# Projection pieces cut into single products between runs of scores, and one and a half value units in each run

## The chip, the core and the metric

The kernel runs on one core of a Trainium2 chip. The metric is the time of one execution on the device, in microseconds; lower is better. Before the change the median of three runs is 2965.22 us (2965.06 to 2965.87).

## The reference

Two layers, each of two parts, are applied to 2048 tokens of width 512, in fp32. The first part is attention with 32 query heads of width 16 that share one key head and one value head; the second sends the two tokens with the highest router score through a gated network and adds a layer norm of everything else.

```python
def _A_ref(x, wq, wk, wv, wo):
    q = (x @ wq).reshape(B, S, H, Dh).transpose(0, 2, 1, 3)
    k, v = x @ wk, x @ wv
    p = softmax(einsum("bhqd,bkd->bhqk", q, k) * Dh ** -0.5)
    return einsum("bhqk,bkd->bhqd", p, v).transpose(0, 2, 1, 3).reshape(B, S, H * Dh) @ wo

x = x + _A_ref(_layernorm(x), ...)          # layer 1
x = x + _B_ref(_layernorm(x), ...)          # two routed tokens through the gated network
x = x + _A_ref(_layernorm(x), ...)          # layer 2
x = x + _B_ref(_layernorm(x), ...)
```

## The kernel before

A layer is a stream of 512 steps. The 2048 tokens make four chunks of 512, the 32 heads make four groups of eight; a chunk and a group make one `p` (16 of them, 32 steps each), and each `p` has two units `u` of 16 steps. A unit is cut into blocks of query columns: two blocks of 8 steps for most units, four blocks of 4 steps for the first and the last unit of a layer (`cuts[u]`).

In each step the recording loop at the end of `layer` issues, for engine PE, four score matmuls of 512 columns (`scores`, L356), whose exponential ACT takes (L358), and four matmuls for the row maxima of queries that come 12 steps later (`max_mm`, L307), which DVE reduces (L309). Scores have three PSUM banks (`psS`), maxima four (`psM`), and the sum of values one (`psO`, tile `pO`).

Every three scores make a run (`RUN`). At the end of a run PE gets the value units that are ready (`pv_mm`, L375): a unit is the product of the exponentials of two scores with the values, four matmuls side by side of 32 output rows each, 256 columns wide. Since two scores make a unit, the runs have one and two units in turn. Behind them stands the held work whose step has come (`run(held.pop(0))`): `at(step, f, ...)` enters it in a table by step, and it is issued whole. fp32 matmuls show twice in the trace, so a unit is eight instructions there.

The projections are such held work. A query piece (`q_piece`) makes 128 tokens of the next `p`'s queries: four products (of four matmuls each, `by_columns`, L154) are summed in a score bank, ACT copies the sum to `qf` (L251), and GpSimd splits it into two parts for `q_stack`, which SP then sends to where scores and maxima read it. An output piece (`o_piece`) makes 128 by 128 of the output projection in the same way, four products from four head groups, and GpSimd adds it to the residual (L457, L458). Query pieces stand at steps 2 to 11 of each `p`; the 16 output pieces of a chunk at steps 14 to 28 of two consecutive `p` of the next chunk. When a chunk's pieces are done, statistics (`stats2`, L178), `norm2` on GpSimd, and `block_b` (L488, L491 on DVE, L493 on GpSimd) follow, and in the first layer the next layer's keys and values.

When a unit's block is summed, ACT copies it out of `pO` (L379). `z_move` to `z_mul` then carry the row sums through DRAM and divide by them. ACT, DVE and GpSimd take their work strictly in the order in which it was recorded.

Of the kernel before, what the change touches and what calls it, by code (L numbers as in the profile page):

```python
# [16 lines left out]
P = 128  # L17
# [35 lines left out]
def interleaved_layers(ctx, tc, x_in, wq, wkv, wo, w_r, w_gate, w_up, w_down, out):  # L53
# [95 lines left out]

    def by_columns(out, lhsT, rhs, start, stop):  # L150

        for j in range(4):
            r = slice(32 * j, 32 * (j + 1))
            nc.tensor.matmul(out[r], lhsT[:, r], rhs, start=start, stop=stop)  # L154

# [91 lines left out]
    def q_piece(G, w):  # L247
        q_proj(G, w)
        qh, ql = (a[:, w] for a in parts[G])
        qf = work.tile([P, P], F32, name="qf")  # L250
        nc.scalar.activation(qf, pqs.pop(G), AF.Copy, scale=DH ** -0.5)  # L251
        nc.gpsimd.tensor_copy(qh, qf)  # L252
        nc.gpsimd.tensor_tensor(ql, qf, qh.bitcast(F32), op=OP.subtract)  # L253

    def q_stack(G, s, w=slice(0, CW), parts_of=range(2 * NSLOT)):
        u = 2 * G + s
        if u not in q_st:
            q_st[u] = work.tile([P, 2, CW], FR, name="q_st", bufs=5)
        for i in parts_of:
            n, h = divmod(i, 2)  # L260
            r = s * HR + h * 32
            nc.sync.dma_start(q_st[u][h * HR + n * DH:h * HR + (n + 1) * DH, :, w].bitcast(F32),
                              parts[G][Q_SLOTS[n]][r:r + 32, w].bitcast(F32))

    def layer(li, src_d, dst_d, changed):
# [93 lines left out]

        def pv_mm(hs):  # L360
# [7 lines left out]
            if r == b == i == 0:  # L368
                po[u] = psO.tile([P, CW], F32, name="pO")
                so[u] = work.tile([P, CW], F32, name=f"so{u % 2}", bufs=6 - 5 * (u % 2))  # L370
            p = pr.pop(hs).rearrange("p h (k j n) -> p h k j n", k=nk, j=2)
            for k in range(nk):
                kt = r * nq + i * nk + k
                for j in range(4):
                    nc.tensor.matmul(po[u][32 * j:32 * (j + 1), b * w:(b + 1) * w],  # L375
                                     v_ext[:, kt, 1 - u % 2:33 - u % 2], p[:, j % 2, k, j // 2, :],
                                     start=kt == 0, stop=kt == KT - 1)
            if r == KT // nq - 1 and i == 1:
                nc.scalar.copy(so[u][:, b * w:(b + 1) * w], po[u][:, b * w:(b + 1) * w])  # L379
                return True  # L380
            return False

        zt, zc, on, on_last = {}, {}, {}, {}
# [34 lines left out]
        def z_last(i):  # L418
# [9 lines left out]
            if u not in zt:  # L428
                zt[u] = work.tile([P, CW], F32, name="so0", bufs=6)
            o = zt[u][:, w]  # L430
# [23 lines left out]
        def o_piece(i, w, gs):  # L454
            o_proj(i, w, gs)
            y = work.tile([P, OW], F32, name="qf")
            nc.scalar.copy(y, py.pop(i))  # L457
            nc.gpsimd.tensor_tensor(x1[i][:, w], x1[i][:, w], y, op=OP.add)  # L458

# [57 lines left out]
        for p in range(NCH * NG):  # L517
            e = 32 * p
            if p + 1 < NCH * NG:
                for n in range(4):  # L520
                    w = slice(n * P, (n + 1) * P)
                    at(e + T_Q + n * D_Q, q_piece, p + 1, w)
                for n in range(2 * NSLOT):
                    s, k = divmod(n, NSLOT)
                    at(e + T_ST + n, q_stack, p + 1, s, slice(0, CW), range(2 * k, 2 * k + 2))
                at(e + T_ST + 2 * NSLOT, parts.pop, p + 1)
            if p == 0:
# [8 lines left out]
            at(e + T_Z + 8, z_spread, u, range(2, 4))  # L536
            at(e + T_Z + 10, z_mul, u)

            if c == NCH - 1 and g == NG - 2:
                for n in range(4 * TPC):  # L540
                    i = c * TPC + n // 4
                    w = slice(n % 4 * OW, (n % 4 + 1) * OW)
                    if n % 4 == 0:
                        at(e + 4, load_x, i)
                    at(e + 14 + n, o_piece, i, w, range(NG - 1))
            if g < NG - 1:
                continue
            for n in range(TPC * 4):
                i = c * TPC + n // 4
                w = slice(n % 4 * OW, (n % 4 + 1) * OW)  # L550
                t = e + 32 * (n // 8) + T_O[n % 8]
                if n % 4 == 0:
                    at(e + 4, load_x, i)
                at(t, o_piece, i, w, range(NG))
                if n % 4 == 3:
                    at(t + 3, stats2, i)
            at(e + T_B[0] - 2, norm2, c)
            for b in range(TPC):
                i = c * TPC + b
                t = e + T_B[0] + T_B[1] * b  # L560
                at(t, block_b, i, nc.vector)
                at(t + 2, store_xl, i)
                at(t + 4, store_x, i)
                if li == 0:
                    t = e + T_N[0] + T_N[1] * b
                    at(t, next_x, i)
# [6 lines left out]
        def load_wd(n):  # L573
            rows = w_down[n * 2 * FS:(n + 1) * 2 * FS, :].rearrange("(k p) d -> p k d", p=FS)
            if n < 4:
                w = work.tile([P, 2, D], F32, name="q_st", bufs=5)
                nc.sync.dma_start(w[:FS], rows)
                wd.extend(w[:FS, k, :] for k in range(2))
            else:
                for k in range(2):  # L580
                    if n < 6:
# [21 lines left out]
        last = NU * KT  # L603
        for n in range(3):
            at(last - 24, load_wd, n)
        at(last - 24, load_wg, 0)
        at(last - 14, load_wd, 3)
        for n in range(4, 8):
            at(last - 13, load_wd, n)
# [32 lines left out]
        for t in range(-LEAD0, last):  # L642
# [5 lines left out]
            for i in range(4):  # L648
# [15 lines left out]
        while ready < 2 * last:  # L664
            pv_mm(ready)
            ready += 1
        while held:
# [7 lines left out]
        for k in range(1, NDC):  # L675
            load_wg(k)
        z_last(TPC - 1)
        finish_b(i - 1)
        o_proj(i, slice(0, D), [NG - 1])
        if nxt:  # L680
# [222 lines left out]
```

## Time and profile before

| | |
|---|---|
| median of three runs | 2965.22 us |
| the profiled execution's own time | 2968.59 us |
| its span, first to last instruction | 2966.5 us |
| mean granted TensorE clock | 0.971 |
| PE busy | 2879.7 us, 97% |
| DVE busy | 2669.2 us, 90% |
| ACT busy | 2295.9 us, 77% |
| GpSimd (POOL) busy | 378.8 us, 13% |

Matmuls are pipelined and their ends are modelled, so PE's busy time says little about how near it is to its limit; the starts of its groups say more. PEld is the weight load. In a table of stretches the columns after the stretch are the busy times of PE, PEld, DVE, ACT and POOL with their instruction counts, the granted clock, the share of the DMA engines and GB/s. In a timeline the first number is the start and the second the length of a merged group of `x` instructions.

### The profile page before, as it was taken

Reading aid. Unit: us, or ns where it says so; the run is one execution under the profiler, and the core shown is the slowest. Engines: PE = TensorE matmul, PEld = TensorE weight load, DVE = VectorE, ACT = ScalarE, POOL = GpSimd, SP = SyncE. Lnnn points to the kernel's source line nnn. Section 1 sums busy time; section 2 is a strip of 40 time slices with the busy share of each in tenths; the row PEclk is TensorE's granted clock in tenths of the full one; section 3 lists DMA queues with packets and bytes.
Section 4 is the critical chain, followed back from the end, with each engine's and each line's share of the span. In section 5 each row is a group of like instructions: output and inputs, shape, how many; then the busy total and the mean of one; then the engine's idle time right before and its main releaser. Section 6 shows DMA issues by size and latency. Waiting matters only on the chain. (4 is left out here: it accounts for less than half of the span.)

```text
span 2966.5 us, 82864 instructions
## 1 busy us (share of the span) xinstructions
PE 2879.7 (97%) x34503; PEld 1502.9 (51%) x34503; DVE 2669.2 (90%) x4616; ACT 2295.9 (77%) x4757; POOL 378.8 (13%) x973
## 2 busy tenths in 40 slices
PE   7999999999999999999979999999999999999997
PEld 4644445544555445544636444455445554455454
DVE  6999999998999999999559999999999999999993
ACT  2788888878888788887717888888788887888783
POOL 3000000121010211111320000001101111011102
PEclk8899999999999999999969999999999999999998
DMA  4000010010100101001310000100101001100122
GB/s 153 13 19 19 10 31 15 19 44 19 33 8 19 43 17 33 19 14 62 89 47 13 19 19 11 30 16 18 45 19 33 19 8 45 31 17 19 36 80 82
DMA packets 65046, 95.18 MB, mean 32 GB/s; under 512 B 21284, under 2 KB 25444, under 8 KB 64672
## 3 DMA queue, kind: packets, MB, share of 16 engines
q1 hardware_dynamic: 62224, 84.10, 9.9%
q8 instruction: 271, 4.44, 0.6%
q10 hardware_dynamic: 2256, 5.77, 0.6%
q14 instruction: 103, 0.84, 0.1%
q0 software_dynamic: 192, 0.03, 0.0%
HBM read 41.93 MB, written 17.77 MB: 20 GB/s over the span
## 5 line engine op out<-in xcount | busy, mean ns | idle before, releaser
L309 DVE TENSOR_REDUCE mx<-pM 128x1 f32<-128x512 f32 x4096 | 2508.0, 682 | 159.1 <-PE pM L307 141.2
L358 ACT ACTIVATE pr<-pS 128x512 f32<-128x512 f32 x4044 | 2105.2, 600 | 331.9 <-PE pM L307 256.3
L307 PE MATMUL pM<-k_st,q_st 48*128 48x512 f32 x4096 | 1478.8, 456 | 17.1 <-DVE mx L309 11.4
L356 PE MATMUL pS<-q_st,k_st 50*128 50x512 f32 (+1 forms) x4248 | 1427.0, 432 | 9.5 <-DMA q_st<-mr 5.7
L375 PE MATMUL pO<-pr,v_ext 128*32 128x256 f32 (+1 forms) x17408 | 1179.8, 377 | 0.0
L356 PEld LDWEIGHTS pS<-q_st,k_st 50*128 50x128 f32 x4248 | 701.9, 187 | 674.3 <-ACT pr L358 519.5
L307 PEld LDWEIGHTS pM<-k_st,q_st 48*128 48x128 f32 x4096 | 697.0, 188 | 69.0 <-DVE mx L309 57.7
L375 PEld LDWEIGHTS pO<-pr,v_ext 128*32 128x32 f32 x17408 | 422.2, 109 | 510.6 <-issue 367.9
L322 POOL CAST mp<-ma 128x8 fp32r<-128x8 f32 (+1 forms) x136 | 25.9, 191 | 1060.7 <-DVE ma L317 502.7
L252 POOL CAST qh<-qf 128x128 fp32r<-128x128 f32 x120 | 34.8, 290 | 802.6 <-ACT qf L251 778.4
L154 PE MATMUL pS<-wo_sb,so 128*32 128x128 f32 (+1 forms) x3888 | 133.9, 277 | 0.0
L154 PE MATMUL pS<-xT,wq_sb 128*32 128x128 f32 x3904 | 133.5, 278 | 0.0
L154 PEld LDWEIGHTS pS<-xT,wq_sb 128*32 128x32 f32 x3904 | 109.8, 111 | 20.8 <-issue 2.7
L458 POOL TENSOR_TENSOR x<-x,qf 128x128 f32<-128x128 f32 x128 | 58.8, 460 | 480.7 <-ACT qf L457 480.7
L154 PEld LDWEIGHTS pS<-wo_sb,so 128*32 128x32 f32 x3888 | 110.4, 110 | 18.3 <-ACT pr L358 0.2
L251 ACT ACTIVATE qf<-pS 128x128 f32<-128x128 f32 x120 | 33.3, 277 | 73.1 <-PE pS L154 73.1
L457 ACT COPY qf<-pS 128x128 f32<-128x128 f32 x128 | 34.3, 268 | 63.3 <-PE pS L154 61.0
L331 ACT COPY mr<-pM 16x128 f32<-16x128 f32 (+1 forms) x136 | 33.2, 244 | 48.4 <-PE pM L329 47.4
L493 POOL TENSOR_TENSOR x<-x,xh 128x512 f32<-128x512 f32 x32 | 52.1, 1627 | 96.9 <-DVE xh L488 96.9
L379 ACT COPY so<-pO 128x256 f32<-128x256 f32 (+1 forms) x136 | 50.8, 373 | 13.8 <-PE pO L375 11.9
L253 POOL TENSOR_TENSOR ql<-qf,qh 128x128 fp32r<-128x128 f32 x120 | 55.1, 459 | 9.6
L329 PEld LDWEIGHTS pM<-ident,mp 128*16 128x16 f32 (+1 forms) x136 | 11.8, 87 | 53.9 <-issue 51.8
(183 smaller groups left out, 716.9 us busy)
## 6 DMA issues: line engine op xcount, KB each, us to landing
q_st<-qh SPq DMA_DIRECT2D x252, 64.0 KB
q_st<-mr SPq DMA_DIRECT2D x512, 2.0 KB
xl_d<-xh SPq DMA_DIRECT2D x32, 256.0 KB
q_st<-ql SPq DMA_DIRECT2D x126, 64.0 KB
zt<-zr_d SPq DMA_DIRECT2D x120, 64.0 KB
pr<-in_w_gate ACTq DMA_DIRECT2D x12, 448.0 KB
x<-in_x SPq DMA_DIRECT2D x16, 256.0 KB
x_d<-x SPq DMA_DIRECT2D x16, 256.0 KB
```

Of the source, the lines that this page charges most:

```text
L154: nc.tensor.matmul(out[r], lhsT[:, r], rhs, start=start, stop=stop)
L252: nc.gpsimd.tensor_copy(qh, qf)
L253: nc.gpsimd.tensor_tensor(ql, qf, qh.bitcast(F32), op=OP.subtract)
L307: nc.tensor.matmul(pm, q_st[u][r, j, q:q + P], k_st[r, c * CW:(c + 1) * CW], start=True, stop=True)
L309: nc.vector.reduce_max(mx[u][:, c, i:i + 1], pm, axis=AX.X)
L356: nc.tensor.matmul(ps[:, k * 2 * w:(k + 1) * 2 * w], k_st[rows, kt * P:(kt + 1) * P], q_st[u][rows, :, b * w:(b + 1) * w], start=True, sto ...
L358: nc.scalar.activation(pr[hs][:, h, :], ps, AF.Exp)
L375: nc.tensor.matmul(po[u][32 * j:32 * (j + 1), b * w:(b + 1) * w], v_ext[:, kt, 1 - u % 2:33 - u % 2], p[:, j % 2, k, j // 2, :], start=kt ...
L379: nc.scalar.copy(so[u][:, b * w:(b + 1) * w], po[u][:, b * w:(b + 1) * w])
L457: nc.scalar.copy(y, py.pop(i))
L458: nc.gpsimd.tensor_tensor(x1[i][:, w], x1[i][:, w], y, op=OP.add)
L493: nc.gpsimd.tensor_tensor(x1[i], x1[i], xl, op=OP.add)
```

## The change

The pieces become lists of steps. `q_piece` and `o_piece` return four functions, one product each, and a last one that copies the sum out and splits or adds it. `whole` issues all of them at once, as before; `put` enters a piece for one block, and `between` issues one step of it behind the value units of each run of that block. Its sum is collected in columns of `pO` that belong to the unit's other block, which has either been copied out or not begun. It takes no score bank. At the end of the block what is left of its pieces is issued before `pO` is copied.

Value units are cut in halves. A run takes `HALVES = 3` halves, that is one and a half units: a whole unit of 256 columns and half of another one, 128 columns wide. If the backlog is larger than four, it takes four halves.

Query pieces are spread over the four blocks of 8 steps from 24 steps before a `p` to its start. Of the 16 output pieces of a chunk, two are issued whole, and 14 are spread over the next 128 steps, one in each block; the later parts of the chunk follow at step 142 and not at 78 (98 for the third chunk). The last chunk's pieces cover two head groups and not three, and stand earlier; its four closing projections cover two groups and not one. The second half of a query stack goes out at step 29 of a `p` and not at 16. `q_st` has four buffers and not five, `so0` eight and not six. Some loads of the gated network's weights move by some steps.

```diff
 RUN = 3
-T_Q, D_Q, T_ST = 2, 3, 13
+HALVES = 3
+T_Q, D_Q, T_ST = 2, 3, (13, 29)
-T_O = (14, 16, 18, 20, 22, 24, 26, 28)
-T_B = (78, 2)
-T_N = (86, 4)
...
+        def between(u, b, all_of=False):
+            pieces = beside.get((u, b), [])
+            nq = cuts[u]
+            while pieces:
+                n, piece, a, state = pieces[0]
+                if state is None:
+                    state = pieces[0][3] = [*piece(*a), 0]
+                q = (1 - b) * CW // 2 + n * P if nq == 2 else (b + 2) % 4 * P
+                out = po[u][:, q:q + P]
+                steps, done, k = state
+                steps[k](out, False, k == len(steps) - 1, True)
+                state[2] += 1
+                if state[2] == len(steps):
+                    done(out)
+                    pieces.pop(0)
+                if not all_of:
+                    break
...
-                    at(e + T_Q + n * D_Q, q_piece, p + 1, w)
+                    if p == 0:
+                        at(T_Q + n * D_Q, whole, q_piece, 1, w)
+                    else:
+                        put(e - 24 + 8 * n, q_piece, p + 1, w)
...
+            if c < NCH - 2:
+                at_once, blocks, tb = (14, 20), range(16, 128, 8), 142
+            elif c == NCH - 2:
+                at_once, blocks, tb = (14, 21, 28, 35, 42), [*range(16, 72, 8), 72, 72, 80, 80], 98
+            else:
+                e -= 32 * 2
+                gs = range(2)
+                at_once, blocks = (15, 18, 21, 24, 27, 30), [24, 24, 32, 32, 40, 40, 48, 52, 56, 60]
...
-            at(e + 3, o_proj, i, slice(0, D), [NG - 1])
+            at(e + 2, o_proj, i, slice(0, D), [NG - 2, NG - 1])
...
-                    while 2 * ready + 1 <= n - RUN and not done:
-                        done = pv_mm(ready)
-                        ready += 1
+                    left = (n - RUN + 1) // 2 * 2 - ready
+                    left = min(left, HALVES + (left > HALVES + 1))
+                    while left > 0 and not done:
+                        halves = range(ready % 2, 2) if left > 1 else range(ready % 2, ready % 2 + 1)
+                        done = pv_mm(ready // 2, halves)
+                        ready += len(halves)
+                        left -= len(halves)
+                    if ready and not done:
+                        between(*at_block[0])
```

How the order moves on PE, in the first layer, where a query piece is made. Names: `pM` and `pS` are the banks of maxima and scores, `pO` the bank of value sums, `xT` and `wq_sb` the operands of a query piece. Before:

```order
L307 MATMUL pM<-k_st_118,q_st 128x512
L375 MATMUL pO<-pr,v_ext_116 32x256 x8
L154 MATMUL pS<-xT,wq_sb 32x128 x16
L356 MATMUL pS<-q_st,k_st_118 128x512
L307 MATMUL pM<-k_st_118,q_st 128x512
```

Now, at such a piece (here L375 is the score, L326 the maximum, L404 the value unit, L153 the product):

```order
L404 MATMUL pO<-pr,v_ext_116 32x256 x4
L404 MATMUL pO<-pr,v_ext_116 32x128 x4
L153 MATMUL pO<-xT,wq_sb 32x128 x4
L375 MATMUL pS<-q_st,k_st_118 128x512
L326 MATMUL pM<-k_st_118,q_st 128x512
L375 MATMUL pS<-q_st,k_st_118 128x512
L326 MATMUL pM<-k_st_118,q_st 128x512
L375 MATMUL pS<-q_st,k_st_118 128x512
L326 MATMUL pM<-k_st_118,q_st 128x512
L404 MATMUL pO<-pr,v_ext_116 32x128 x4
L404 MATMUL pO<-pr,v_ext_116 32x256 x4
L153 MATMUL pO<-xT,wq_sb 32x128 x4
```

Sixteen matmuls of a piece stood behind two units; now four stand behind one and a half, in each of four runs, and they go to `pO`.

The second place is the end of a query piece on PE, with the semaphores that an instruction waits for. Before, the piece itself waits for a score bank, and the value units of the next run wait for nothing:

```order
L375 MATMUL pO<-pr,v_ext_116 32x256 x4
L154 MATMUL pS<-xT,wq_sb 32x128 [waits Activation_49]
L154 MATMUL pS<-xT,wq_sb 32x128 x15
L356 MATMUL pS<-q_st,k_st_118 128x512 [waits Activation_49]
L307 MATMUL pM<-k_st_118,q_st 128x512 [waits DVE_49]
L356 MATMUL pS<-q_st,k_st_118 128x512 [waits Activation_49]
L307 MATMUL pM<-k_st_118,q_st 128x512 [waits DVE_49]
L356 MATMUL pS<-q_st,k_st_118 128x512 [waits Activation_49]
L307 MATMUL pM<-k_st_118,q_st 128x512 [waits DVE_49]
L375 MATMUL pO<-pr,v_ext_116 32x256 x8
```

Now:

```order
L153 MATMUL pO<-xT,wq_sb 32x128 x4
L375 MATMUL pS<-q_st,k_st_118 128x512 [waits Activation_49]
L326 MATMUL pM<-k_st_118,q_st 128x512 [waits DMAHW4_49,DMAHW6_49,DMAHW0_49,DVE_49]
L375 MATMUL pS<-q_st,k_st_118 128x512 [waits Activation_49]
L326 MATMUL pM<-k_st_118,q_st 128x512 [waits DMAHW5_49,DMAHW7_49,DMAHW3_49,DVE_49]
L375 MATMUL pS<-q_st,k_st_118 128x512 [waits Activation_49]
L326 MATMUL pM<-k_st_118,q_st 128x512 [waits DVE_49]
L404 MATMUL pO<-pr,v_ext_116 32x256 [waits Activation_49]
L404 MATMUL pO<-pr,v_ext_116 32x256 x3
```

The wait for ACT has moved from the piece to the value unit of the run behind its last product, which may not write `pO` before ACT has copied the piece out of it. In the whole program 352 matmuls of value units wait for ACT now, and 128 before.

More of the change, by code (lines that the diff above doesn't have):

```diff
@@ L148, in aux, with by_columns, whole @@
         return a
-    def by_columns(out, lhsT, rhs, start, stop):
+    def by_columns(out, lhsT, rhs, start, stop, shared=False):
         for j in range(4):
             r = slice(32 * j, 32 * (j + 1))
-            nc.tensor.matmul(out[r], lhsT[:, r], rhs, start=start, stop=stop)
+            nc.tensor.matmul(out[r], lhsT[:, r], rhs, start=start, stop=stop, skip_group_check=shared)
+    def whole(piece, *a):
+        steps, done = piece(*a)
+        out = aux([P, P], F32)
+        for n, f in enumerate(steps):
+            f(out, n == 0, n == len(steps) - 1, False)
+        done(out)
     def bank():
@@ L247, in q_piece, with step, f, done @@
     def q_piece(G, w):
[L248 to L253, printed above, removed]
+        c, g = divmod(G, NG)
+        def step(k):
+            def f(out, *flags):
+                by_columns(out, wq_sb[:, k, g * P:(g + 1) * P], xT[:, k, c * CW + w.start:c * CW + w.stop], *flags)
+            return f
+        def done(out):
+            if G not in parts:
+                parts[G] = [work.tile([P, CW], FR, name=n) for n in ("qh", "ql")]
+            qh, ql = (a[:, w] for a in parts[G])
+            qf = work.tile([P, P], F32, name="qf")
+            nc.scalar.activation(qf, out, AF.Copy, scale=DH ** -0.5)
+            nc.gpsimd.tensor_copy(qh, qf)
+            nc.gpsimd.tensor_tensor(ql, qf, qh.bitcast(F32), op=OP.subtract)
+        return [step(k) for k in range(NDC)], done
     def q_stack(G, s, w=slice(0, CW), parts_of=range(2 * NSLOT)):
@@ L257, in q_stack @@
         if u not in q_st:
-            q_st[u] = work.tile([P, 2, CW], FR, name="q_st", bufs=5)
+            q_st[u] = work.tile([P, 2, CW], FR, name="q_st", bufs=4)
         for i in parts_of:
@@ L381, in pv_mm, with put @@
             return False
+        beside, at_block = {}, [None]
+        def between(u, b, all_of=False):
[11 more added lines that the diff above has]
+                if state[2] == len(steps):
+                    done(out)
+                    pieces.pop(0)
+                if not all_of:
+                    break
+        def put(step, piece, *a):
+            u, r = divmod(step, KT)
+            b, r = divmod(r, KT // cuts[u])
+            assert r == 0, step
+            p = beside.setdefault((u, b), [])
+            p.append([len(p), piece, a, None])
+            assert len(p) <= (2 if cuts[u] == 2 else 1), (u, b)
         zt, zc, on, on_last = {}, {}, {}, {}
@@ L454, in o_piece, with step, f, done @@
         def o_piece(i, w, gs):
[L455 to L458, printed above, removed]
+            c, b = divmod(i, TPC)
+            def step(g):
+                def f(out, *flags):
+                    by_columns(out, on[c * NG + g][:, b * P:(b + 1) * P], wo_sb[:, g, w], *flags)
+                return f
+            def done(out):
+                y = work.tile([P, OW], F32, name="qf")
+                nc.scalar.copy(y, out)
+                nc.gpsimd.tensor_tensor(x1[i][:, w], x1[i][:, w], y, op=OP.add)
+            return [step(g) for g in gs], done
         def key(i):
@@ L574, in load_wd @@
             rows = w_down[n * 2 * FS:(n + 1) * 2 * FS, :].rearrange("(k p) d -> p k d", p=FS)
-            if n < 4:
-                w = work.tile([P, 2, D], F32, name="q_st", bufs=5)
+            if n < 3:
+                w = work.tile([P, 2, D], F32, name="q_st", bufs=4)
                 nc.sync.dma_start(w[:FS], rows)
@@ L603, in layer @@
         last = NU * KT
-        for n in range(3):
+        for n in range(2):
             at(last - 24, load_wd, n)
[L606 to L609, printed above, removed]
+        for n in range(2, 8):
+            at(last - 14 + n // 2, load_wd, n)
+        at(last - 10, load_wg, 0)
         for b in range(TPC - 1):
```

86 lines of the change are left out of this document (49 added, 37 removed).

## The prediction

> **What bounds the kernel now.** I read the shares of busy time first, then the groups of instructions, then the stretches.
>
> ```profile
> PE 2879.7 (97%) x34503; PEld 1502.9 (51%) x34503; DVE 2669.2 (90%) x4616; ACT 2295.9 (77%) x4757; POOL 378.8 (13%) x973
> L309 DVE TENSOR_REDUCE mx<-pM 128x1 f32<-128x512 f32 x4096 | 2508.0, 682 | 159.1 <-PE pM L307 141.2
> 200.00:400.00 200.00, 198.96 (x2178) 95.01 (x2178) 194.53 (x331) 170.90 (x348) 12.82 (x37) 1.00 0.08 18
> 1000.00:1200.00 200.00, 199.00 (x2330) 100.94 (x2329) 185.59 (x314) 165.73 (x348) 20.83 (x53) 1.00 0.08 24
> ```
>
> Two engines look full. DVE has nearly all its time in the 4096 row maxima, and most of its idle time is waiting for the matmul that makes the next one (141.2 us). In the third row (columns: stretch, then busy time of PE, PEld, DVE, ACT, POOL) DVE is 97% busy; in the fourth, where the output pieces run as well, 93%. Since a pipelined PE reads as busy while it waits, I price it by the starts of its runs instead:
>
> ```profile
> 1749.08 0.50 PE L356 MATMUL pS<-q_st,k_st 50*128 50x512 f32 x1
> ...
> 1749.98 0.64 PE L375 MATMUL pO<-pr,v_ext 128*32 128x256 f32 x8
> 1750.55 0.50 PE L356 MATMUL pS<-q_st,k_st 50*128 50x512 f32 x1
> ...
> 1751.67 1.07 PE L375 MATMUL pO<-pr,v_ext 128*32 128x256 f32 x16
> 1752.67 0.50 PE L356 MATMUL pS<-q_st,k_st 50*128 50x512 f32 x1
> ...
> 1753.58 0.64 PE L375 MATMUL pO<-pr,v_ext 128*32 128x256 f32 x8
> 1754.04 1.06 PE L154 MATMUL pS<-xT,wq_sb 128*32 128x128 f32 x32
> 1755.02 0.50 PE L356 MATMUL pS<-q_st,k_st 50*128 50x512 f32 x1
> ```
>
> A run is three scores and three maxima (0.90 us from 1749.08 to 1749.98), then one value unit (0.57, to 1750.55) or two (1.00, from 1751.67 to 1752.67), then held work. So a light run is 1.47, a heavy one 1.90; the heavy one here took 2.12, because its maxima part was held up to 1.12 by full banks. A whole projection piece adds 1.44 - 0.57 = 0.87, about 0.22 for each of its four products. DVE's price for three maxima, and what it does besides, once per chunk of 128 steps:
>
> ```profile
> 2105.32 0.54 DVE L488 TENSOR_SCALAR xh<-x,mv,rs 128x512 f32<-128x512 f32 x1
> 2105.95 1.82 DVE L491 SCALAR_TENSOR_TENSOR zt<-xh,wr_sb 128x512 f32<-128x512 f32 x1
> ...
> 2107.69 5.46 DVE L309 TENSOR_REDUCE mx<-pM 128x1 f32<-128x512 f32 x9
> ...
> 2113.65 0.69 DVE L491 SCALAR_TENSOR_TENSOR zt<-xh,wr_sb 128x512 f32<-128x512 f32 x1
> ```
>
> Nine maxima in 5.46 with a last one of 0.68 make 0.597 apart, 1.79 for a run. The four `block_b` of a chunk (0.54 + 0.69 each, the first 0.54 + 1.82) add some 6 us in a clump of 8 steps. The same instruction in the next chunks gives what a chunk takes now:
>
> ```profile
> 976.82 1.26 DVE L488 TENSOR_SCALAR xh<-x,mv,rs 128x512 f32<-128x512 f32 x1
> 1331.14 1.24 DVE L488 TENSOR_SCALAR xh<-x,mv,rs 128x512 f32<-128x512 f32 x1
> 2448.90 0.54 DVE L488 TENSOR_SCALAR xh<-x,mv,rs 128x512 f32<-128x512 f32 x1
> 2793.87 0.54 DVE L488 TENSOR_SCALAR xh<-x,mv,rs 128x512 f32<-128x512 f32 x1
> 1725.38 0.28 PE L329 MATMUL pM<-ident,mp 128*16 128x128 f32 x1
> 1725.59 0.50 PE L356 MATMUL pS<-q_st,k_st 50*128 50x512 f32 x1
> ```
>
> The second layer takes 344.3 us a chunk (344 and 345); the first 354.3, which also makes the next layer's keys and values, 10.0 for four token tiles. The last two rows price a transposed row block at 0.21. PE's own work in a second-layer chunk is 170.7 runs x (0.90 + 0.785) = 287.6, 32 pieces x 0.87 = 27.8 and 16 transposes x 0.21 = 3.4: 319. DVE's is 512 x 0.597 = 306 and the 6 of the clump, with some 8 of small work: 320. So two engines with 320 us of work each take 344. Neither is the bound alone; what costs is that they take turns at being late. The check: I add up, over the 10.67 runs of an 8-step block, the larger of PE's time and DVE's 1.79. By the order, pieces stand three to one behind light runs: 3.83 light at 1.79, 4.83 heavy at 1.90, 1.5 light with a piece at 2.34, 0.5 heavy with one at 2.77, 0.21: 21.15. Sixteen blocks and 5 for the clump (6 less what PE was behind anyway) are 343.4, measured 344.3. **The uneven runs explain the overhang.**
>
> **The change part by part.** *Even runs and spread products.* No matmul work is added: the same columns stream, 1.5 units cost 0.785 above the maxima part, a product 0.22. By the order of the change, a full block of 10.67 runs holds about seven even runs with a product (1.91), one with two units and a product (0.90 + 1.00 + 0.22 = 2.12), 1.67 even ones without (1.69, so DVE's 1.79), and one short one at a block's end (half a unit or one, again 1.79). With the transpose: 13.37 + 2.12 + 2.99 + 1.79 + 0.21 = 20.48; sixteen of them and 5 for the clump, which keeps its spacing, are 332.7. That is 10.7 less than the same rule gives before. PE's own sum is 319, so 8 us of this are excess that a run-ahead can take up: four banks against three maxima a run leave one maximum, 0.6 us, and the new differences (0.1 to 0.5) fit in it where the old ones (0.9 for a piece) did not. I take half, 4; the ends, none and all 8, stay in the range.
>
> *Evictions from the value bank.* In the order 352 value units wait for ACT against 128. ACT's copy of a piece stands behind the run's three exponentials:
>
> ```profile
> 2870.26 0.49 PE L356 MATMUL pS<-q_st,k_st 50*128 50x512 f32 x1
> ...
> 2870.79 3.05 ACT L358 ACTIVATE pr<-pS 128x512 f32<-128x512 f32 x6 [0.55 <-PE pM L307]
> L251 ACT ACTIVATE qf<-pS 128x128 f32<-128x128 f32 x120 | 33.3, 277 | 73.1 <-PE pS L154 73.1
> L379 ACT COPY so<-pO 128x256 f32<-128x256 f32 (+1 forms) x136 | 50.8, 373 | 13.8 <-PE pO L375 11.9
> PEld pO L375 <- ACT so L379: 17.7, 57, 0.4
> PEld pS L356 <- ACT qf L251: 26.2, 112, 0.5
> PEld pS L356 <- ACT qf L457: 24.2, 102, 0.8
> ```
>
> Exponentials start 0.53 after the run and stand 0.49 apart, so the third ends at 2.1, which is 0.2 into the next run when a run is 1.91. The 0.28 copy ends at about 0.5, the value sums come at 0.90: no wait. Behind a half-unit run (0.90 + 0.36 = 1.26) the copy `so` starts at 0.84 and ends at 1.22, 0.3 to 0.4 late, as 57 did for 0.31 each after light runs. Some 40 such ends more against fewer light ones: 1.5 us a chunk; none to 3 for the range. The Trainium skill's page "PSUM — Partial Sum Buffer" (section Terms) says that an engine reading a bank while TensorE writes that bank and quadrant is a collision, so these waits cannot be dropped; by it every eviction shuts the value sums out for its 0.28 us, and 210 of them would be 59 us. The sum here doesn't use that, since the trace has the maxima part lying over the copy. What ends is that a piece holds one of three score banks: the last two rows, 50 us of weight loads waiting. I count nothing, since the run behind the piece above started its maxima part at once; at most 10.
>
> *Queues.* The second half of each query stack goes 13 steps later on SP, five steps (12 us) before its first maximum; before it was eighteen.
>
> ```profile
> 2274.11 1.24 SPq L262 DMA_DIRECT2D q_st<-qh  x2
> ```
>
> Six issues of 0.62 and a landing fit. If SP were held by the row DMAs ahead, PE would wait at the maximum and DVE with it; all 30 stacks would have to be 2.6 us late to eat the gain. POOL has 13% and one 1.6 us `block_b` sum at a time; two `qf` buffers cover it.
>
> *The sum.* Output pieces run from step 128 to about 472, 2.69 chunks a layer, 5.38 in all, each 10.7 + 4 - 1.5 = 13.2 less: 71. The first 128 steps have query pieces alone; DVE idles 5.5 of 200 there (third row above), 9 in 320 us, and half of that twice is 9. The end of a layer:
>
> ```profile
> 2891.84 0.66 PE pS L154 x24
> L154 PE MATMUL pS<-wo_sb,so 128*32 128x512 f32 x48 | 6.2, 592 | 0.0
> ```
>
> There PE alone paces: twelve pieces of 0.66 become eight products (7.9 - 1.8), but four closing projections take a second head group (6.2 / 6 = 1.03 each): 2 less. In the first layer two tiles of keys and values (10.0 / 4 each) come into it: 3 more. Together 1 more. Sum: 71 + 9 - 1 = 79. The profiled execution has 2968.6 us with a span of 2966.5; it becomes 2889.6 with 2887.5. The median shown, 2965.2, lies 3.4 below that execution: **2886 us**.
>
> **The rivals.** *All the excess is taken up* (0.15): PE paces alone, a chunk falls by 10.7 + 8 = 18.7, 101 in all, the early stretch by 18, the score banks give 10: 2965 - 128 = 2837. For it: heavy runs stretch only because DVE's banks are full. Against: the same rule missed before by 1 us only, though banks were there too.
>
> *Evictions and block ends eat half* (0.15): the 224 new waits cost 0.2 each, 45 us: 2931. For it: the 57 waits of 0.31. Against: ACT has 0.3 us idle in a run of 1.91.
>
> *Slower: every small group pays a start* (0.09). One unit costs 0.57, two 1.00: the first has 0.14 of its own. If each of the 800 products that now stand alone paid that 0.14 for switching weights and columns, 112 us would go against 79: 2998. It decides from 79 / 800 = 0.10 us. Against it: 32 instructions with new weights every eight took 0.87 behind a unit, streaming alone. The page "TensorE: Matmul & The Clock Gate" (Part 3, The mechanism) has weight loads overlap only matmuls of another row group; all of these use the same rows, so by it each load would stand alone. The piece above disagrees, its 32 loads and matmuls starting within 0.98 us.
>
> *It does not do what it says* (0.04): the runs at block ends (0.5, then 2 with a product) and the 38 pieces still whole leave the turns as they are, 2965.
>
> **How the numbers follow.** The forecast has 0.57, its own range 2865 to 2910. For 8 in 10 I reach down to the first rival and up to the second: low 2840, high 2930; the upper unknowns (no run-ahead, 3 a chunk for evictions, nothing early) give 2965 - 5.38 x 7.7 + 1 = 2925. Faster by over 0.2%, about what a measurement here can tell, 0.57 + 0.15 + 0.15 = 0.87; within it 0.04; slower 0.09.
>
> **What would show it.** In the changed profile a run with a product should be 1.9 us from first score to first score, with its value part at 1.00 (0.79 + 0.22). A chunk between first `block_b` instructions shifts in step, so I read busy shares: DVE should rise from 93% to 96% in the full stretches, its wait for the maxima matmul from 141 to below 90. If value units wait for `qf` by more than 30 us in the list of waits, the second rival holds; if a run with one product is over 2.05, the third. Wrong altogether if DVE waits for the query stack.

## The result, and the profile after

The changed kernel takes **2880.73 us** (median of four runs, 2879.23 to 2882.73), 0.9715 of the time before (95% interval 0.9698 to 0.9732); the forecast was 2886, in a range of 2840 to 2930. The profiled execution spans 2877.4 us, where it spanned 2966.5, at a mean granted clock of 0.980 (before 0.971). Of all the runs told of here one is left out, of the kernel with three banks for the maxima: it took 3103.66 us at a granted clock of 0.835, where the others of that kernel have 0.976 to 0.977.

The page of the changed kernel, its shares of busy time and its costliest group (L328 is the row maximum, before L309; the score is L375, the exponential L377, the maxima matmul L326, the value unit L404, the product of a piece L153):

```profile
PE 2799.0 (97%) x39431; PEld 1613.9 (56%) x39431; DVE 2665.3 (93%) x4616; ACT 2321.9 (81%) x4757; POOL 377.6 (13%) x973
L328 DVE TENSOR_REDUCE mx<-pM 128x1 f32<-128x512 f32 x4096 | 2509.9, 681 | 85.6 <-PE pM L326 72.4
```

The maxima cost what they did, and DVE's idle time before them has fallen from 159.1 to 85.6 us. The same shows in stretches of the second layer (columns as before: PE, PEld, DVE, ACT, POOL busy, clock, DMA share, GB/s), the first in the changed kernel and then the one between the same times in the kernel before, which holds other steps:

```profile
2300.00:2500.00 200.00, 199.81 (x2924) 113.87 (x2928) 195.89 (x331) 174.53 (x356) 18.00 (x52) 1.00 0.07 17
```

```profile
2300.00:2500.00 200.00, 198.41 (x2361) 100.47 (x2361) 187.87 (x323) 160.46 (x329) 25.79 (x57) 0.97 0.09 25
```

DVE goes from 94 to 98%, ACT from 80 to 87%. (Over a whole chunk of the second layer, from first `block_b` to first `block_b`, DVE is busy 324.5 of 343.6 us before and 323.4 of 329.7 now, the same 94 and 98%.) A run of the changed kernel with one product, in the timeline:

```profile
2301.81 0.49 PE L375 MATMUL pS<-q_st,k_st 50*128 50x512 f32 x1
...
2302.71 0.86 PE L404 MATMUL pO<-pr,v_ext 128*32 128x128 f32 x16
...
2303.39 0.40 PE L153 MATMUL pO<-wo_sb,so 128*32 128x128 f32 x8
...
2303.72 0.49 PE L375 MATMUL pS<-q_st,k_st 50*128 50x512 f32 x1
```

Values start 0.90 after the scores and the run lasts 1.91; over all such runs from 1900 to 2800 us the median is 1.910, and 1.695 without a product. The first `block_b` of each chunk gives the chunks:

```profile
765.06 0.53 DVE L560 TENSOR_SCALAR xh<-x,mv,rs 128x512 f32<-128x512 f32 x1
...
1106.07 0.54 DVE L560 TENSOR_SCALAR xh<-x,mv,rs 128x512 f32<-128x512 f32 x1
...
2203.72 0.54 DVE L560 TENSOR_SCALAR xh<-x,mv,rs 128x512 f32<-128x512 f32 x1
...
2533.42 0.54 DVE L560 TENSOR_SCALAR xh<-x,mv,rs 128x512 f32<-128x512 f32 x1
```

A chunk takes 341.0 us in the first layer (354.3 before) and 329.7 in the second (344.3): 13.3 and 14.6 less.

Where the 89 us of the spans come from, by the starts of the exponentials, which number the steps (both layers together, us; the forecast's column is its own sum, laid out by the same steps):

| steps | before | after | difference | forecast |
|---|---|---|---|---|
| 0 to 128 | 664.3 | 654.8 | -9.5 | -9 |
| 128 to 448 | 1743.2 | 1680.7 | -62.5 | -66 |
| 448 to 511 | 356.1 | 345.9 | -10.2 | -4 |
| between the layers | 85.4 | 81.7 | -3.7 | 0 |
| before the first step and after the last | 117.5 | 114.3 | -3.2 | 0 |

### The profile page after: what moved, and what is told of

Read it like the earlier page. It is cut to its first block, busy times and chain, and to the rows that moved or that the text cites. A ratio compares the mean times of both kernels' runs of the same rounds, so it can differ in the third digit from the quotient of the medians.

```text
span 2877.4 us, 92955 instructions
## 1 busy us (share of the span) xinstructions
PE 2799.0 (97%) x39431; PEld 1613.9 (56%) x39431; DVE 2665.3 (93%) x4616; ACT 2321.9 (81%) x4757; POOL 377.6 (13%) x973
## 5 line engine op out<-in xcount | busy, mean ns | idle before, releaser
L328 DVE TENSOR_REDUCE mx<-pM 128x1 f32<-128x512 f32 x4096 | 2509.9, 681 | 85.6 <-PE pM L326 72.4
L377 ACT ACTIVATE pr<-pS 128x512 f32<-128x512 f32 x4044 | 2139.4, 602 | 334.1 <-PE pM L326 242.4
L326 PE MATMUL pM<-k_st,q_st 48*128 48x512 f32 x4096 | 1409.3, 445 | 13.6 <-DVE mx L328 7.8
L375 PE MATMUL pS<-q_st,k_st 50*128 50x512 f32 (+1 forms) x4248 | 1370.1, 422 | 10.8 <-DMA q_st<-mr 5.2
L404 PE MATMUL pO<-pr,v_ext 128*32 128x128 f32 (+1 forms) x22528 | 1176.1, 328 | 1.3 <-ACT so L410 1.0
L375 PEld LDWEIGHTS pS<-q_st,k_st 50*128 50x128 f32 x4248 | 683.6, 187 | 447.2 <-ACT pr L377 247.7
L404 PEld LDWEIGHTS pO<-pr,v_ext 128*32 128x32 f32 x22528 | 562.7, 109 | 547.6 <-issue 355.5
L326 PEld LDWEIGHTS pM<-k_st,q_st 48*128 48x128 f32 x4096 | 669.2, 187 | 63.0 <-DVE mx L328 51.5
L153 PE MATMUL pO<-xT,wq_sb 128*32 128x128 f32 x3584 | 180.0, 273 | 0.0
L153 PE MATMUL pO<-wo_sb,so 128*32 128x128 f32 x2816 | 141.4, 273 | 0.0
L153 PEld LDWEIGHTS pO<-xT,wq_sb 128*32 128x32 f32 x3584 | 111.0, 110 | 31.2
L153 PEld LDWEIGHTS pO<-wo_sb,so 128*32 128x32 f32 x2816 | 87.6, 110 | 28.5
L410 ACT COPY so<-pO 128x256 f32<-128x256 f32 (+1 forms) x136 | 51.5, 379 | 4.5 <-PE pO L404 4.4
L478 POOL TENSOR_TENSOR so<-so,zt 128x512 f32<-128x512 f32 x30 | 38.6, 1286 | 1.2 <-DMA zt<-zr_d 1.2
L153 PE MATMUL pS<-wo_sb,so 128*32 128x128 f32 (+1 forms) x864 | 38.1, 309 | 0.0
```

Source lines behind the costliest of these rows:

```text
L326: nc.tensor.matmul(pm, q_st[u][r, j, q:q + P], k_st[r, c * CW:(c + 1) * CW], start=True, stop=True)
L328: nc.vector.reduce_max(mx[u][:, c, i:i + 1], pm, axis=AX.X)
L375: nc.tensor.matmul(ps[:, k * 2 * w:(k + 1) * 2 * w], k_st[rows, kt * P:(kt + 1) * P], q_st[u][rows, :, b * w:(b + 1) * w], start=True, sto ...
L377: nc.scalar.activation(pr[hs][:, h, :], ps, AF.Exp)
L404: nc.tensor.matmul(po[u][32 * j:32 * (j + 1), b * w + q.start:b * w + q.stop], v_ext[:, kt, 1 - u % 2:33 - u % 2], p[:, j % 2, k, j // 2, ...
L478: nc.gpsimd.tensor_tensor(a, a, zt[u][:, w], op=OP.mult)
```

## The experiments

The first theory was the prediction's: TensorE and VectorE (PE and DVE in the profile) take turns at being late, and the even runs end that. Each time below is a median; the ratio is to the kernel before on the same chip. On the chips used the kernel before took 2965.3 to 2968.4 us, so a difference between rows of two chips is uncertain by some 3 us.

### Each part alone

| kernel | median, us | ratio (95%) |
|---|---|---|
| before, with one and a half units between runs | 2932.05 | 0.9885 (0.9869 to 0.9902) |
| changed, pieces at once in a score bank | 2932.56 | 0.9884 (0.9868 to 0.9901) |
| changed, pieces at once in the value bank | 2928.1 | 0.9870 (0.9853 to 0.9886) |
| changed, whole units (one and two in turn) | 2894.59 | 0.9756 (0.9740 to 0.9772) |
| changed | 2880.73 | 0.9715 (0.9698 to 0.9732) |

**Whole units again**, in the changed kernel:

```diff
-                    left = min(left, HALVES + (left > HALVES + 1))
...
-                        halves = range(ready % 2, 2) if left > 1 else range(ready % 2, ready % 2 + 1)
-                        done = pv_mm(ready // 2, halves)
-                        ready += len(halves)
-                        left -= len(halves)
+                        done = pv_mm(ready // 2, range(2))
+                        ready += 2
+                        left -= 2
```

> The changed kernel with value units uncut, so that runs have one and two units in turn again; products stay spread. Theory (turns: a run costs the larger of PE's time and DVE's 1.79): of a full block's eight runs with a product four cost 1.79 (0.90 + 0.57 + 0.22 = 1.69) and four 2.12; with the rest 20.76 against 20.48 with even runs, 4.5 us a chunk, 24 us in all, less if one maximum of run-ahead takes some of it up: 2890 to 2910 us. Rival (all of the gain comes from spreading the pieces, or from the score bank that they no longer hold): within 4 us of the changed kernel, 2877 to 2885.

**Pieces at once in the value bank**, in the changed kernel: all four products of a piece and its copy behind one run.

```diff
-                steps[k](out, False, k == len(steps) - 1, True)
-                state[2] += 1
-                if state[2] == len(steps):
-                    done(out)
-                    pieces.pop(0)
+                for k in range(len(steps)):
+                    steps[k](out, False, k == len(steps) - 1, True)
+                done(out)
+                pieces.pop(0)
```

> The changed kernel with even runs, but a piece's products issued all at once in the first runs of its block, still summed in the value bank. Theory (turns): two runs of a block cost 1.69 + 0.87 = 2.56 and the others DVE's 1.79, 20.85 against 20.48 in a block, 6 us a chunk, some 32 us in all: 2905 to 2920 us. Rival (the gain comes from the freed score bank, since the weight loads of scores waited 50 us for the copies of pieces before): no loss, 2877 to 2885. Rival (even units alone bring the gain): no loss either.

**Pieces at once in a score bank**: the same, through `whole`.

```diff
...
-                steps, done, k = state
-                steps[k](out, False, k == len(steps) - 1, True)
...
+                whole(piece, *a)
+                pieces.pop(0)
```

> As the run before it, with the sum in a score bank as in the kernel before. Theory (turns): the bank counts nothing, the same time as with the value bank within 5 us, 2905 to 2925. Rival (score bank): the sum in the value bank costs nothing and this one 30 to 50 us more.

**The kernel before with even units**: only the recording loop and `pv_mm` of the change.

```diff
-                    while 2 * ready + 1 <= n - RUN and not done:
-                        done = pv_mm(ready)
-                        ready += 1
+                    left = (n - RUN + 1) // 2 * 2 - ready
+                    left = min(left, HALVES + (left > HALVES + 1))
+                    while left > 0 and not done:
+                        halves = range(ready % 2, 2) if left > 1 else range(ready % 2, ready % 2 + 1)
+                        done = pv_mm(ready // 2, halves)
+                        ready += len(halves)
+                        left -= len(halves)
...
```

> The kernel before with value units cut in halves, one and a half in each run, and nothing else changed. Theory (turns): pieces stand behind runs of 1.69, so two runs of a full block cost 2.56 and the others 1.79: 20.85 against 21.15 in a block, 5 us a chunk, 26 us in all: 2930 to 2950. Rival (spreading alone): no change, 2960 to 2970.

Whole units and the kernel before with even units came out within the theory's ranges. Both kernels with pieces at once lie 8 us above theirs, so spreading the products is worth 47 us where the theory had 32.

From before to the changed kernel the steps are: even units, 35; the pieces' new places and the rest of the change, nothing in sum; the value bank in place of a score bank, 4; the spreading of the products, 47. The score bank's 4 us stand in the list of waits of the kernel with pieces at once in it, as score loads that wait for the pieces' copies (the changed kernel has 6.4 for the first of them):

```profile
PEld pS L375 <- ACT qf L519: 24.4, 114, 0.2
PEld pS L375 <- ACT qf L268: 24.2, 106, 0.2
```

So 49 us of weight loads that wait cost 4 us of time. The even units do not add up: without the spreading they give 35, with it only 14 (12 by the ratios). Two edits that each lengthen the shortest runs share part of what they gain.

### What else moved

**`block_b` four steps apart in the kernel before, and three in the changed kernel.**

```diff
-T_B = (78, 2)
+T_B = (78, 4)
```

> The kernel before with the four block_b of a chunk four steps apart and not two, nothing else changed. The clock rows show five stretches of 7 to 10 us at half clock in the middle of the stream of the kernel before, each just behind the first block_b of a chunk, and one of 3.4 us in the changed kernel. Theory (turns): they cost little, DVE being the later one there; 0 to 8 us less, 2957 to 2966. Rival (clock): a good part of the 85 us that the change brought is these stretches, 44 us in all at half clock; without them 2940 to 2950.

```diff
-                t = e + tb + 2 * b
+                t = e + tb + 3 * b
```

> The changed kernel with the block_b of a chunk three steps apart and not two. Theory (turns): DVE has some 6 us more than PE there whatever the spacing, since PE has hardly any idle time in a full stretch; 0 to 6 us less, 2875 to 2881. Rival (clock): no stretch at half clock is left to be gained but one of 3.4 us, 0 to 2 us.

Before: 2968.48 us, 1.0008 (0.9999 to 1.0017), nothing. Of the 44 us at half clock 34 stand in this run too, so it does not take the rival's cause away; in sum the spacing is worth nothing there. The trace of the kernel before prices the stretches. These are the 16 steps from the first `block_b` of each chunk on, in its second layer; a stretch of 6.8 us at half clock falls into the first, one of 10.2 us into the second, none into the third:

```profile
2104.98:2150.96 45.98, 44.60 (x392) 20.27 (x394) 44.68 (x79) 34.50 (x70) 7.43 (x8) 0.93 0.21 65
2447.93:2495.21 47.28, 46.04 (x392) 21.02 (x386) 44.79 (x79) 34.62 (x69) 7.45 (x8) 0.89 0.20 63
2792.52:2836.67 44.15, 42.19 (x384) 19.75 (x386) 43.92 (x78) 34.40 (x70) 7.43 (x8) 1.00 0.21 67
```

They take 1.8 and 3.1 us more than the third. Up to 1 us of that may be other work: with half maxima (below), where no such stretch falls into them, the three take 39.7, 39.2 and 38.7. So a stretch costs some 1 to 3 us, and, if those of the first layer cost as much, the clock has some 5 to 15 of the 85 us. That is an estimate from these rows; no run takes the stretches away alone.

The changed kernel: 2895.03, 0.9755 (0.9742 to 0.9768), 14 slower (12 by the ratios), which neither theory had. The steps 480 to 496 of each layer took 5.1 us more, and the timeline of VectorE shows why:

```profile
2798.23 0.69 DVE L563 SCALAR_TENSOR_TENSOR zt<-xh,wr_sb 128x512 f32<-128x512 f32 x1 [2.88 <-POOL so L478]
```

The fourth `block_b` of the third chunk now falls among the divisions of `z_mul` (L478), which read the one `zt` buffer that it writes: VectorE stands 2.88 us for GpSimd, with all maxima behind. A stretch of 6.8 us at half clock follows at step 493 of both layers, where the changed kernel has none. Together they are 10 of the 14 us; the rest was not traced. It is a mishap of this spacing and says nothing of the clump.

**Three banks for the maxima and four for the scores**, in the changed kernel, and **each copy of a piece made twice**.

```diff
-    psM = ctx.enter_context(tc.tile_pool(name="psM", bufs=4, space=bass.MemoryType.PSUM))
-    psS = ctx.enter_context(tc.tile_pool(name="psS", bufs=3, space=bass.MemoryType.PSUM))
+    psM = ctx.enter_context(tc.tile_pool(name="psM", bufs=3, space=bass.MemoryType.PSUM))
+    psS = ctx.enter_context(tc.tile_pool(name="psS", bufs=4, space=bass.MemoryType.PSUM))
```

> The changed kernel with three banks for maxima and four for scores, in place of four and three. Theory (turns with one maximum of run-ahead): PE can no longer be a maximum ahead; the 8 us of a chunk between PE's own time and the larger of the two in each run show in full and a little more, 20 to 60 us: 2900 to 2940. Rival (the larger of the two counts in each run already, and run-ahead takes up nothing): within 5 us of 2881.

```diff
-            nc.scalar.activation(qf, out, AF.Copy, scale=DH ** -0.5)
+            for _ in range(2):
+                nc.scalar.activation(qf, out, AF.Copy, scale=DH ** -0.5)
...
-                nc.scalar.copy(y, out)
+                for _ in range(2):
+                    nc.scalar.copy(y, out)
```

> The changed kernel with ACT's copy of each piece out of its bank made twice, one behind the other, which leaves the value bank 0.28 us later and more. Theory (the copy lies beside the next run's scores and maxima): it ends at 0.5 us into the next run now and 0.8 then, the value units come at 0.90: 0 to 10 us more, 2881 to 2891. Rival (evictions): the 210 value units behind a copy each wait by its whole length, 59 us more: 2930 to 2945.

Three maxima banks: 3007.86, 1.0140 (1.0122 to 1.0159), 127 slower than the changed kernel and well past the theory's 2900 to 2940. The direction was right and the size was not. Its list of waits, the maxima's loads waiting for VectorE and VectorE waiting for the maxima (51.5 and 72.4 in the changed kernel):

```profile
DVE mx L328 <- PE pM L326: 133.5, 366, 3.2
PEld pM L326 <- DVE mx L328: 116.5, 392, 1.3
```

With only as many banks as a run has maxima, most runs wait for VectorE, even those with a product: from 1900 to 2800 us they last 2.02 in the median, where they lasted 1.91. The fourth bank is what gives the "one maximum" of run-ahead that the prediction speaks of.

Copies twice: 2896.49, 0.9762 (0.9749 to 0.9775), 16 slower: above the theory's 2881 to 2891, far below the rival's 2930 to 2945. In its timeline (two copies, then the value loads, in a run that starts its scores at 2303.35):

```profile
2303.54 0.56 ACT L529 COPY qf<-pO 128x128 f32<-128x128 f32 x2
...
2304.25 0.37 PEld L405 LDWEIGHTS pO<-pr,v_ext 128*32 128x32 f32 x12 [0.37 <-ACT qf L529]
```

The value part still starts 0.90 into the run, and so it does in the median of all runs from 1900 to 2800 us that hold such copies, so even the doubled copy does not shut the value sums out. The cost is some 0.06 us for each of the 248 copies (210 out of the value bank, 38 out of a score bank). It shows in other runs: full runs with neither a copy nor a product start their values at 1.04 in the median, where the changed kernel has 0.94. That fits ACT's own time in front of later exponentials, which was not traced further. It was the first sign that ACT stands nearer to the limit than the prediction had it.

### Is VectorE the other engine?

If the turns are with VectorE, halving its price must bring both kernels to the same time. In both, each maximum was taken over 256 of the 512 keys:

```diff
-            nc.vector.reduce_max(mx[u][:, c, i:i + 1], pm, axis=AX.X)
+            nc.vector.reduce_max(mx[u][:, c, i:i + 1], pm[:, :CW // 2], axis=AX.X)
```

> The kernel before, with each maximum taken over the first 256 of its 512 keys only (the maxima matmuls stay whole), so that VectorE's price of a run of three, 1.79 us, falls to some 0.9 to 1.1 and is never the larger of the two. Left out: half of the keys in the maxima. Theory (the 85 us are turns between TensorE and VectorE): TensorE sets every run in both kernels, by the sum of its own parts; the kernel before falls to 2800 to 2850 us. Rival (the change takes away work or waits of TensorE's own, such as evictions or the score bank's order): the kernel before gains as much as the changed one does, and the two stay 60 to 85 us apart.

> The changed kernel with the same cut of the maxima to 256 keys. Left out: half of the keys in the maxima. Theory: 2800 to 2840 us, within 15 us of the kernel before with the same cut, since nothing is left that the even runs could level. Rival: 60 to 85 us below the kernel before with the same cut.

Before 2892.74 us, 0.9747 (0.9730 to 0.9763); changed 2816.97, 0.9489 (0.9473 to 0.9505). They stay **76 us apart**. The first theory falls as it was put: of the 85 us, at most some 10 go when VectorE's price is halved. The page and the waits of the kernel before with half maxima:

```profile
PE 2809.9 (97%) x34503; PEld 1459.1 (50%) x34503; DVE 1664.0 (58%) x4616; ACT 2290.2 (79%) x4757; POOL 381.0 (13%) x973
...
PEld pS L356 <- ACT pr L358: 547.3, 1512, 1.1
...
PEld pM L307 <- DVE mx L309: 9.8, 15, 1.7
```

VectorE is 58% busy and the maxima wait for it 9.8 us in all, yet heavy runs still start their values 1.07 us into the run (median from 1900 to 2800 us) and not 0.90. The first of the two waits names the other engine, ACT. It was in the list of the kernel before as well, and in the very run that the prediction had quoted as held "by full banks" (scores at 1750.55, values at 1751.67). The prediction does not show these rows of its timeline:

```profile
PEld pS L356 <- ACT pr L358: 519.5, 1407, 0.9
```

```profile
1749.61 3.05 ACT L358 ACTIVATE pr<-pS 128x512 f32<-128x512 f32 x6 [0.39 <-PE pM L307]
...
1751.24 0.18 PEld L356 LDWEIGHTS pS<-q_st,k_st 50*128 50x128 f32 x1 [0.30 <-ACT pr L358]
```

Here is the mechanism. The light run began at 1749.08. Its exponentials start 0.53 later and stand 0.51 apart, so the third ends 2.1 us after the run began, and the third score of the next run, which needs that bank, loads its weights at 2.16. An undisturbed run would have loaded them 0.22 earlier (values at 0.90, here at 1.12). The light run lasts 1.47; with 1.69 nothing would have waited. **Three score banks set a shortest run of some 1.7 us, beside VectorE's 1.79.** (The expectation below reckoned 1.56, by the exponential's end against the third score's matmul; the load stands earlier than the matmul.)

The rule of the larger of two prices, with 1.70 in place of 1.79 and no clump, gives 20.8 us for a block before and 20.2 after, 9 a chunk apart. Steps 192 to 320, a chunk long, take 335.1 and 326.9 us in the second layer with half maxima, and 345.1 and 337.0 in the first: 8 apart.

**A fourth score bank** with the half maxima, in the kernel before:

```diff
-    psM = ctx.enter_context(tc.tile_pool(name="psM", bufs=4, space=bass.MemoryType.PSUM))
-    psS = ctx.enter_context(tc.tile_pool(name="psS", bufs=3, space=bass.MemoryType.PSUM))
+    psM = ctx.enter_context(tc.tile_pool(name="psM", bufs=3, space=bass.MemoryType.PSUM))
+    psS = ctx.enter_context(tc.tile_pool(name="psS", bufs=4, space=bass.MemoryType.PSUM))
```

> The kernel before with the maxima over half of the keys, and one bank moved from the maxima to the scores (three and four, where it was four and three). Left out: half of the keys in the maxima. The two runs with halved maxima stayed 76 us apart (2893 and 2817), with VectorE nowhere near its limit, so the first theory, turns with VectorE, does not carry. Second theory: with three score banks the third score of a run waits for the third exponential of the run before, which ends 0.53 + 3 x 0.52 = 2.1 us after that run began, so a run cannot be shorter than about 1.56 us, and a light run of 1.47 makes the next one wait 0.1 to 0.2 us; a fourth bank takes that away, and the time falls by 50 to 75 us to 2820 to 2845 us, with the waits of score weight loads for exponentials well below half of 547 us. Rival (the difference is in TensorE's own work or in what the pieces do): the time stays at 2880 to 2895 us.

2833.27 us, 0.9549 (0.9533 to 0.9565): 59 below the same kernel with three score banks, and 16 above the changed one with half maxima. The waits, and a heavy run behind a light one (scores at 2303.21, after a light run that began at 2301.74):

```profile
PEld pS L356 <- ACT pr L358: 263.8, 703, 1.0
```

```profile
2303.21 0.50 PE L356 MATMUL pS<-q_st,k_st 50*128 50x512 f32 x1
...
2304.16 1.07 PE L375 MATMUL pO<-pr,v_ext 128*32 128x256 f32 x16
```

Still one and two units in turn, still whole pieces, and values at 0.95. Over all heavy runs without a piece from 1900 to 2800 us the median start of the values goes from 1.07 to 0.91, and the median run from 2.07 to 1.91, which is TensorE's own price. So 59 us, of the 76 by which the two kernels differ, go with the score banks' run-ahead, of which the 4 for the bank that a piece holds may be part. What a fourth bank would give the changed kernel with half maxima was not tried. The waits fell to 48%, not the "well below half" that was expected: part of this row is no cost, being the gap of some 0.2 us at a run's first load.

**Spreading the products**, with half maxima: the kernel with pieces at once in the value bank, cut in the same way.

```diff
-            nc.vector.reduce_max(mx[u][:, c, i:i + 1], pm, axis=AX.X)
+            nc.vector.reduce_max(mx[u][:, c, i:i + 1], pm[:, :CW // 2], axis=AX.X)
```

> The changed kernel with each piece issued whole in the value sums' bank (the second of the runs above with that edit: 2928 us, 47 above the changed kernel), and with the maxima over half of the keys. Left out: half of the keys in the maxima. If the 47 us of spreading the products are turns with VectorE (a run of 1.69 us without a piece is shorter than VectorE's 1.79), they go with VectorE's price: 2815 to 2830 us, as the changed kernel with halved maxima has 2817. If they are turns with the exponentials, or TensorE's own price of a whole piece, 30 to 50 us stay: 2847 to 2867 us.

2830.27 us, 0.9537 (0.9521 to 0.9553): the spreading is worth 13 here, and 47 with whole maxima; the time lies just above the 2815 to 2830 that turns with VectorE alone would leave. With pieces at once and whole maxima VectorE's wait for the maxima matmul was back near the 141 of the kernel before:

```profile
DVE mx L328 <- PE pM L326: 139.0, 227, 3.9
```

So both engines, ACT by the score banks and VectorE by its own price, stand behind the 85 us, one behind the other, beside the 5 to 15 of the clock. Even units take light runs from 1.47 to 1.69, which nearly clears the score banks; a run of 1.69 is still below VectorE's 1.79, so VectorE takes back part of it, until a product brings most runs to 1.91, above both. By these runs even units, places and value bank are worth 62 without VectorE's limit and 39 with it, the spreading 13 and 47.

## Why the prediction was right or wrong

**Prices of runs: right.** 1.910 measured against 1.91 with a product, 1.695 against 1.69 without, values at 0.90.

**The rule (the larger of two engines' prices, run by run): near in size, partly by luck, and wrong in the engine.** The rule alone gave 10.7 a chunk; 13.2 came of it with 4 for run-ahead and less 1.5 for evictions. The chunks show 13.3 and 14.6, of which some 1 to 3 are the half-clock stretches, a term that the sum did not have. No run measures the 4 by itself, so a match within 1.4 us is partly luck. And the sentence "its maxima part was held up to 1.12 by full banks" took the banks to be VectorE's; in that run it was a score bank and ACT. The sum came out because the limit of the score banks, 1.7, happens to lie 0.09 under VectorE's 1.79: the wrong one gave nearly the right overhang, and its check (343.4 against 344.3) could not tell the two apart. The step that failed was reading the group of maxima and its idle time, and not the load that waited inside the run. The numbers were in hand: "the third ends at 2.1" was set only against a run of 1.91, where it is harmless, and never against one of 1.47.

**Half of the 8 us taken up (4 a chunk): not tested by itself.** Steps 128 to 448 came in at 62.5 where the forecast's sum had 66. The three-bank run shows that losing one maximum of run-ahead costs 127 us; what the change gains by it stays open.

**Evictions, 1.5 a chunk: the waits grew as forecast, but they are not what held the runs; the test named for them was bad.** Copies that hold value loads show so in the changed kernel's waits:

```profile
PEld pO L404 <- issue: 355.5, 1092, 0.7
PEld pO L404 <- ACT qf L268: 36.9, 101, 0.4
PEld pO L404 <- ACT so L410: 26.0, 101, 0.8
```

The wait for `qf` passed the 30 us that were to mean the second rival. It is no cost: each is 0.37, the ordinary gap ahead of a value load is 0.33 ("issue"), and the run quoted above (2301.81), which has such a wait, still starts its values at 0.90. The waits for `so` grew by 8.3 (from 17.7), as 1.5 a chunk had it. But behind a half-unit run, where the prediction had the values wait for `so`, the trace shows the score banks again. Here that run is 2001.65 to 2002.92, and the next one starts its values at 1.33:

```profile
2003.63 0.39 ACT L410 COPY so<-pO 128x256 f32<-128x256 f32 x1
2003.81 0.18 PEld L375 LDWEIGHTS pS<-q_st,k_st 50*128 50x128 f32 x1 [0.30 <-ACT pr L377]
...
2004.24 0.59 PEld L404 LDWEIGHTS pO<-pr,v_ext 128*32 128x32 f32 x16 [0.24 <-ACT so L410]
```

The values come 0.43 behind the third score's load, as in the run at 1750.55 (1751.24 to 1751.67), and the copy had ended at 2004.02. The 0.3 to 0.4 us of lateness was right, then, and its cause was not.

By the Trainium skill's "PSUM — Partial Sum Buffer" (Terms) a copy out of a bank while TensorE writes the same bank and quadrant is a collision, so the two must take turns. If each of these turns cost the length of its copy, 59 us would have gone, as the prediction had estimated. Nothing here speaks against the rule, but the turns were free, since the copy lies over the maxima part: runs from 1900 to 2800 us that hold a piece's copy start their values at 0.90 in the median.

**Score bank, nothing to 10: right**, 4, for what a piece's hold of a bank costs beside even units. What three score banks cost light runs without any piece, the sum had nowhere.

**The early 128 steps, 9: right**, 9.5.

**The ends of the layers: wrong in sign.** The forecast had the closing steps cost 1 more, on top of what was left of the chunks' gain, 5: 4 less in all. They give 10.2. The sum put the keys and values of two tiles into the end of the first layer and left out what leaves steps 448 to 480 there: the third chunk's clump, with a stretch of 6.8 us at half clock, and tiles of keys and values. These steps fall from 93.1 to 84.9 us, though output pieces of the last chunk stand in them now. Steps 480 to 511, to which the clump and the tiles went, change by +1.3 there and by -0.9 in the second layer. The 3.7 between the layers and the 3.2 around the stream were not in the sum; how far they belong to the change was not tried.

**The rivals.** All the excess taken up (2837) did not come: the changed kernel still gains 64 us when the maxima are halved, so VectorE still holds it. Evictions eating half (2931) falls with the waits above. A start for every product (2998) falls with the run of 1.91: 0.22 for a product alone, as within a piece. The rule of the Trainium skill's "TensorE: Matmul & The Clock Gate" (Part 3, The mechanism), by which loads overlap running matmuls only where the row group differs, is not borne out: eight loads and eight matmuls of the same rows lengthen a run from 1.695 to 1.910, and the eight loads alone are busy 0.25 us.

**DVE from 93 to 96%, its wait below 90:** measured 98% and 72.4. Both tests held and neither tested the cause: VectorE gets busier whichever wait goes, since its work is the same in a shorter time.

## What to carry to other kernels

Work out for each pair of producer and consumer the shortest run that its banks allow: when the last consumer of one run is done, less when the next run needs that bank. Where two such limits lie close together, easing one gains only down to the other, and a model with the wrong one of them can still match the total; halving one consumer's work tells them apart. Open the waits inside one slow run before naming the engine that holds it.

## What the runs showed of the hardware that was not expected

- One bank moved from the maxima to the scores costs the changed kernel 127 us. With half maxima the same move gains the kernel before 59.
- A copy of a value bank's columns made twice (0.56 us) costs some 0.06 us a copy, in other runs; the run that holds it still starts its values at 0.90, since they wait for it within a gap that is there anyway.
- A wait in the list can be free: 49 us of score loads behind the pieces' copies were worth 4 us, and 37 us of value loads behind `qf` left the start of the values at 0.90.
- In the second layer of the kernel before, a stretch of 6.8 or 10.2 us at half clock made 16 steps some 1 to 3 us longer, less than half its length.
